# Score tiles in an attention kernel: three in every step, one of them from two half-wide matmuls in one bank, ordered through GpSimd

## The chip, the core and the metric

The kernel runs on one core of a Trainium2 chip. The core has five engines with their own instruction queues: TensorE (PE; its weight loads are listed apart as PEld), VectorE (DVE), ScalarE (ACT), GpSimd (POOL) and SyncE (SP), which here only issues DMAs. PE writes into PSUM, eight banks of 128 partitions by 512 float32; DVE and ACT read it. The metric is device time in microseconds (us), the median of several runs.

## The reference

One input x (2048 tokens by 512 features) is normalised and goes through two branches, which are multiplied and added to x:

```python
xn = _layernorm(x)
qkv = (xn @ wqkv).reshape(B, S, 3, H, Dh).transpose(2, 0, 3, 1, 4)   # H = 32 heads of Dh = 16
scores = einsum("bhqd,bhkd->bhqk", q, k) * Dh ** -0.5
o = einsum("bhqk,bhkd->bhqd", softmax(scores), v)
s = o.transpose(0, 2, 1, 3).reshape(B, S, D) @ wo
g = silu(einsum("bsf,fd->bsd", gelu(xn @ w1 + b1), w2) + b2)          # F = 1376
return x + s * g
```

## The kernel before, in words

All is float32; products with weights are made from a high and a low part, three matmuls in place of one. Attention works on 32 **units** u: eight groups of four heads times four chunks of 512 queries.

The softmax needs each query's largest score first, so each unit's scores are made twice.

- **S tiles** (line 174): 128 queries by 512 keys of one head, one matmul of 48 contraction rows into one bank; DVE takes the row maximum (line 176). 64 S tiles make a unit, 2048 in all. The maxima of a unit are reduced (line 188, `nmh` and `nm`), a low part is subtracted on POOL (line 189), transposed on PE (line 200), copied (line 208) and sent through DRAM into two extra rows of the queries (`load_mh`).
- **T tiles** (line 654): 128 keys by 512 queries with 50 rows, the two extra ones subtracting the maximum; ACT takes the exponential (line 656) out of PSUM.
- **V matmuls** (line 723): the four heads' exponentials times their values, eight instructions that use all four column groups of PE and accumulate over 16 key blocks in one bank. ACT copies that bank to `os` (line 730) at a unit's end; later DMAs, a reciprocal on DVE and a multiply on POOL (`o_div`, line 760) divide by the sum.

Heads come in two kinds, a = 0 and a = 1: their rows lie at partitions 0 and 64. An S or T matmul uses only one half of PE's rows, so two of them, one on each half, run side by side. The V matmuls use all rows.

In the first stage (LayerNorm, projections, the gated MLP) S tiles of the first units are put between other matmuls by `fill`, 4 x LEAD = 560 of them. Then comes a loop of 513 **steps** n, which holds the attention. Step n makes the four T tiles of key block n mod 16 of unit n // 16, the V matmuls of step n - 1, and some S tiles of later units. `due(n)` says how many S tiles are to be made by then; the difference to those made (three, in some steps four, none from about step 492 on) picks a string from ORDER:

```python
ORDER = {0: "TTTTV", 1: "TTTTSV", 2: "TTTSTSV", 3: "STTTSTSV", 4: "STTSTSVTS"}
```

T tiles alternate a = 0, 1, 0, 1; the S tiles take the other half than the tile ahead of them, as long as neither kind is four ahead. The order of work on each engine is the order in which the program writes it; waits between engines follow from the tiles. `todo` (filled by `at`) hangs other work on a step: loads of queries and of the next group's keys (`load_k`, on POOL's queue, `pos=0` being behind the first T of a step, `pos=3` behind the last), `o_move`, `o_den`, `o_div`, the output weights (`load_wo`, `split_wo`), and near the end the output matmuls (`w_mul`, line 77).

PSUM: S tiles use three banks in turn (two of `ps_s`, and whichever of `ps_x` and `ps_v` does not hold the V sum of this unit); T tiles use four (three of `ps_t`, one of `ps_m`). In the first stage S tiles have the two banks of `ps_s`.

`mark` in the first stage shows how two row halves that add into one bank are ordered: an ACT instruction waits for the matmul of the one half, and the matmul of the other half waits for it (`add_manual_dep`).

Of the kernel before, what the change touches and what calls it, by code (L numbers as in the profile page):

```python
# [27 lines left out]
GH = 4  # L28
# [3 lines left out]
VW = DH + 1  # L32
LEAD = 140
NW = 10
# [4 lines left out]
W2B = 2  # L39
ORDER = {0: "TTTTV", 1: "TTTTSV", 2: "TTTSTSV", 3: "STTTSTSV", 4: "STTSTSVTS"}  # L40
KB = 3
# [5 lines left out]
def fused(ctx: ExitStack, tc: tile.TileContext, x, wqk, wv, wo, w1, b1, w2, b2, out):  # L47
# [3 lines left out]
    keep = ctx.enter_context(tc.tile_pool(name="keep", bufs=1))  # L51
    ps_s = ctx.enter_context(tc.tile_pool(name="ps_s", bufs=2, space=PSUM))
    ps_x = ctx.enter_context(tc.tile_pool(name="ps_x", bufs=1, space=PSUM))
# [27 lines left out]

    QS, QT, MX, NM, MH = {}, {}, {}, {}, {}
    qss = []
    NU = NG * NCH

    s_ring = [ps_s, ps_s]
    s_turn = [0]
    end_tile = lambda: s_tile()

    def s_tile(shape=(P, CH)):  # L90
        pool = s_ring[s_turn[0] % len(s_ring)]
        s_turn[0] += 1
        return pool.tile(list(shape), F32, name="pv" if pool is ps_v else "ps")

# [50 lines left out]

    def load_mh(u):
        for a in range(2):
            nc.sync.dma_start(QT[u][64 * a + 48:64 * a + 50].bitcast(F32), mh_d[u, :, a::2, :])

    halves = [[(u, st, p) for u in range(NU) for st in range(NCH * NCH) for p in range(2)] for _ in range(2)]  # L150
    made = [0, 0]
    ended = [0]
    later, errands = [], []

# [4 lines left out]
    def flush():  # L159
        while later and later[0][0] <= 0:  # L160
            u = later.pop(0)[1]
            s_end1(u)
            s_end2(u)

    def s_one(a):
        u, st, p = halves[a][made[a]]
        made[a] += 1
        g = u // NCH
        qi, ki = divmod(st, NCH)
        if u not in MX:  # L170
            MX[u] = qring.tile([P, GH, NCH, NCH], F32, name="mx")
        ps = s_tile()
        r, q = slice(64 * a, 64 * a + 3 * DH), QS[u]
        nc.tensor.matmul(ps, q[r, p, qi * P:(qi + 1) * P],  # L174
                         kts[g % KB][p][r, ki * CH:(ki + 1) * CH], start=True, stop=True)
        nc.vector.tensor_reduce(MX[u][:, 2 * p + a, qi, ki:ki + 1], ps, axis=AX.X, op=OP.max)  # L176
        if min(made) == 32 * (ended[0] + 1):
            v = ended[0]
            ended[0] += 1
            s_end0(v)  # L180
            later.append([12 if "seen" in prog else 8, v])

    def s_end0(u):
        nm = qring.tile([P, GH * NCH], F32, name="nm")
        NM[u] = qring.tile([P, 2, GH * NCH], F32R, name="nmh")
        mx = MX.pop(u).rearrange("p a b c -> p (a b) c")
        for dst in (NM[u][:, 0], nm):
            nc.vector.tensor_reduce(dst, mx, axis=AX.X, op=OP.max, negate=True)  # L188
        nc.gpsimd.tensor_sub(NM[u][:, 1], nm, NM[u][:, 0].bitcast(F32))  # L189
# [8 lines left out]
    def s_end1(u):  # L198
        pm = end_tile()
        nc.tensor.matmul(pm[:2 * GH * NCH, :P], NM.pop(u).rearrange("p i a -> p (i a)"), ident_r, start=True, stop=True)  # L200
        MH[u] = pm

    def s_end2(u):
        mh = qring.tile([2 * GH * NCH, P], F32, name="mh")
# [4 lines left out]
        nc.sync.dma_start(mh_d[u].rearrange("i j (q s) -> (i j q) s", s=P), mh)  # L209

    sa = ExitStack()
# [109 lines left out]
    with ExitStack() as s1:  # L321
# [4 lines left out]
        def a_tile(shape):  # L326
            banks[0] += 1
            i = banks[0] % 6
            if i < 2:
                return ps_s.tile(list(shape), F32, name="ps")  # L330
            if i == 2:
                return ps_x.tile(list(shape), F32, name="ps")
            return ps_t.tile(list(shape), F32, name="pst")
# [139 lines left out]

    SYNC = mybir.DependencyInfo(mybir.DependencyClass.Sync, mybir.DependencyReason.DATA)
    prog.update(n=0, pe=0, seen=0)
# [163 lines left out]
    def t_tile():  # L639
        turns[0] += 1  # L640
        if turns[0] < 5:
            pool = (ps_m, ps_x, ps_s, ps_s)[turns[0] - 1]
# [46 lines left out]
    s_ring.append(ps_x)  # L689
    s_turn[0] = 2  # L690
    qz.close()
# [15 lines left out]

    def split_wo(k):
        nc.gpsimd.tensor_copy(wo_h[:, k], WR[k])
        nc.gpsimd.tensor_sub(wo_l[:, k], WR.pop(k), wo_h[:, k].bitcast(F32))  # L710

    PV, OS, DN, DR = {}, {}, {}, {}
    def pv_pool(u):
        return (ps_v, ps_x)[u % 2]

    def pv_step(u, k):
        g = u // NCH
        if k == 0:
            pool = pv_pool(u)
            PV[u] = pool.tile([P, CH], F32, name="pv" if pool is ps_v else "ps")  # L720
        for j in range(GH):
            h = (g * GH + j) * VW
            nc.tensor.matmul(PV[u][32 * j:32 * j + 32, :], vsb[:, k, h:h + 32], PT[u, k][:, j, :],  # L723
                             start=(k == 0), stop=(k == NT - 1))
        del PT[u, k]
        if k == NT - 1:
            OS[u] = wb.tile([P, CH], F32, name="os", bufs=1)
            pv = PV.pop(u)
            if u < NU - 1:
                nc.scalar.activation(OS[u], pv, AF.Copy)  # L730
# [75 lines left out]
    def w_mul(t, ks, parts=(0, 1)):  # L806
        if t not in PW:
            PW[t] = [ps_t.tile([P, CH], F32, name="pst") if NW <= t < NT - NCH or i else
                     ps_m.tile([P, CH], F32, name="ps") if t == NT - 1 else s_tile()
                     for i, cs in enumerate(cols(t))]  # L810
# [28 lines left out]
    def due(n):  # L839
        return min(4 * L, 4 * LEAD + max(0, (4 * (L - LEAD) * n - 300) // (DONE - 1)))  # L840

    for u in range(NU):
        g, c = divmod(u, NCH)
        if c == 0 and g == KB:
            at(57, load_k, g, range(6), nc.gpsimd, 0, S // 2, pos=0)
            at(64, load_k, g, range(6), nc.gpsimd, S // 2, S // 2, pos=0)
        elif c == 0 and g > KB:
            for i in range(6):
                at(64 * (g - KB + 1) + 6 + i, load_k, g, (i,), nc.gpsimd, pos=0)
        if u >= 2:  # L850
            at(16 * u - 14, load_qt, u)
            need = min(n for n in range(L) if due(n) >= 64 * (u + 1)) + (4 if u < NU - 1 else 2)
            at(max(16 * u - 14, need), load_mh, u)
        if u < NU - 1:
            at(16 * u + 17, o_move, u, pos=0)
            at(16 * u + (25 if g < NG - 1 else 19), o_den, u, pos=0)
            at(16 * u + (31 if g < NG - 1 else 22), o_div, u, nc.gpsimd)
    T3 = range(NT - NCH, NT)
    last, late = 1, range(NW, NT)
    for t in range(NW):  # L860
# [13 lines left out]
    for k in range(KT):  # L874
        at(104 + 16 * k, load_wo, k)
        at(112 + 16 * k, split_wo, k)
    for n in range(L + 1):
        ua, ka = divmod(n, 16)
        want = due(n) - sum(made)
        i = 0  # L880
        if n > 1 and (n - 1) % 16 == 0:
            s_ring[:] = [ps_s, ps_s, pv_pool((n - 1) // 16 + 1)]
            s_turn[0] = 0
        for op in ORDER[want] if n > 1 else ("TTTTV", "TTTVTSS")[n]:
            if op == "S":
                h = 1 - last if made[1 - last] - made[last] < 4 and made[1 - last] < 2 * L else last
                s_one(h)
                last = h
            elif op == "V":
# [68 lines left out]
```

## Time and profile before

| | |
|---|---|
| median of 3 runs | 1640.5 us (1640.18 to 1640.83) |
| the profiled execution | 1640.26 us, of it the profile's span 1638.5 us |
| granted clock of TensorE | 0.999 |
| PE busy | 1627.3 us (99%) |
| DVE busy | 1389.8 us (85%) |
| ACT busy | 1271.9 us (78%) |
| POOL busy | 373.5 us (23%) |
| first V load, last V load | 483.4 us, 1614.0 us |

Rows of a timeline give the start, the length, the engine, the line, the operation, the tile written and the tiles read, and the count of instructions merged into the row; in brackets stands how long the engine was idle before and what ended that. Matmuls are pipelined: a row's length is more than the time until the next can follow, and the ends are modelled. The first stage ends near 483 us; the loop of steps fills most of what follows, and 20 steps without S tiles and the last output tiles make the end.

### The profile page before, as it was taken

The numbers are of one execution on the slowest core, as the hardware profiler recorded it, in microseconds if no ns is written. First come the engines' busy times: TensorE is split into PE (matmuls) and PEld (weight loads), VectorE is DVE, ScalarE is ACT, GpSimd is POOL, SyncE is SP. The second block draws the span as 40 slices with busy tenths as digits, with TensorE's granted clock in tenths as the row PEclk, the third lists the DMA queues.
The fourth block names the chain that finished last, engine by engine and source line by source line (L and its number), as shares of the span: only waits on it lengthen the run. The fifth ranks groups of instructions, "written<-read, shape, count | busy, mean of one in ns | idle before, by whom it ended". The sixth has DMA issues, their size and how long they took to land.

```text
span 1638.5 us, 31026 instructions
## 1 busy us (share of the span) xinstructions
PE 1627.3 (99%) x11656; PEld 898.3 (55%) x11656; DVE 1389.8 (85%) x2299; ACT 1271.9 (78%) x2523; POOL 373.5 (23%) x366
## 2 busy tenths in 40 slices
PE   9999999999999999999999999999999999999998
PEld 7898999988974434333334443433334443434445
DVE  7299999999988888888888888888888888888733
ACT  4333433434349999999999999999999999999984
POOL 4235565756630011001000100100100000000144
PEclk9999999999999999999999999999999999999999
DMA  6625334453330122112301411411141111110152
GB/s 200 147 72 150 113 118 130 138 135 121 111 117 26 29 50 47 31 45 49 61 26 28 79 29 28 66 31 31 36 59 32 28 28 37 32 28 22 56 191 94
DMA packets 76214, 116.83 MB, mean 71 GB/s; under 512 B 24964, under 2 KB 26244, under 8 KB 74696
## 3 DMA queue, kind: packets, MB, share of 16 engines
q1 hardware_dynamic: 72604, 102.42, 22.3%
q0 software_dynamic: 3264, 12.35, 4.5%
q8 instruction: 92, 1.51, 0.4%
q14 instruction: 58, 0.48, 0.1%
q10 hardware_dynamic: 196, 0.07, 0.0%
HBM read 84.35 MB, written 25.97 MB: 67 GB/s over the span
## 4 chain that ended last, share of the span: by engine, by line
PE 94%; DVE 2%; issue 2%; ACT 1%; POOL 1%; DMA 0%; SPq 0%; ACTq 0%; DVEq 0%; POOLq 0%
PE ps L174 23%; PE pv L723 15%; PE ps L723 15%; PE ps L506 12%; PE pst L654 12%; PE pst L506 7%; PE pv L174 3%; PE ps L77 2%; PE pv L506 2%; ACT slot L656 1%; PE pst L77 1%; POOL ol L791 1%; DVE mx L176 0%; PE ps L654 0%; POOL gx L824 0%
## 5 line engine op out<-in xcount | busy, mean ns | idle before, releaser
L176 DVE TENSOR_REDUCE mx<-ps 128x1 f32<-128x512 f32 x1808 | 1168.6, 685 | 160.3 <-PE ps L654 76.6
L656 ACT ACTIVATE slot<-pst 128x512 f32<-128x512 f32 x1533 | 806.9, 608 | 5.0 <-PE ps L174 4.5
L656 ACT ACTIVATE slot<-ps 128x512 f32<-128x512 f32 x515 | 308.7, 600 | 44.4 <-PE ps L654 9.8
L174 PE MATMUL ps<-kt,slot 48*128 48x512 f32 x864 | 327.9, 443 | 0.0
L174 PEld LDWEIGHTS ps<-kt,slot 48*128 48x128 f32 x864 | 158.2, 184 | 256.8 <-DVE mx L176 235.6
L654 PE MATMUL pst<-qt,kt 50*128 50x512 f32 x1149 | 294.1, 409 | 0.4 <-DVE gt L587 0.3
L723 PE MATMUL pv<-slot,vsb 128*32 128x512 f32 x2048 | 272.7, 605 | 0.0
L723 PE MATMUL ps<-slot,vsb 128*32 128x512 f32 x2048 | 272.5, 604 | 0.0
L506 PE MATMUL ps<-slot,w1h 64*128 64x512 f32 x1088 | 225.2, 394 | 0.4 <-ACT junk L519 0.4
L174 PE MATMUL ps<-kt,qz 48*128 48x512 f32 x512 | 211.1, 416 | 0.2
L654 PE MATMUL ps<-qt,kt 50*128 50x512 f32 x387 | 189.8, 492 | 0.0
L176 DVE TENSOR_REDUCE mx<-pv 128x1 f32<-128x512 f32 x240 | 163.8, 683 | 11.6 <-PE ps L654 7.8
L174 PE MATMUL ps<-slot,slot 48*128 48x512 f32 x432 | 166.2, 441 | 0.2
L506 PEld LDWEIGHTS ps<-slot,w1h 64*128 64x128 f32 x1088 | 153.8, 185 | 9.5 <-ACT junk L519 2.3
L654 PEld LDWEIGHTS pst<-qt,kt 50*128 50x128 f32 x1149 | 144.5, 186 | 21.5 <-issue 8.4
L506 PE MATMUL ps<-slot,w1l 64*128 64x512 f32 x544 | 154.0, 393 | 0.0
L174 PEld LDWEIGHTS ps<-slot,slot 48*128 48x128 f32 x432 | 78.6, 184 | 115.0 <-DVE mx L176 104.8
L307 POOL TENSOR_TENSOR hl<-hg,hh 128x512 fp32r<-128x512 f32 x76 | 96.9, 1297 | 129.2 <-ACT hh L306 80.8
L189 POOL TENSOR_TENSOR nmh<-nm,nmh 128x16 fp32r<-128x16 f32 x32 | 7.1, 221 | 497.9 <-DVE nm L188 266.5
L519 ACT ACTIVATE junk<-ident_r 1x1 f32<-1x1 f32 x91 | 17.8, 196 | 120.4 <-PE pst L506 104.0
L174 PEld LDWEIGHTS ps<-kt,qz 48*128 48x128 f32 x512 | 93.7, 183 | 11.8 <-DVE mx L176 2.7
L654 PE MATMUL pst<-qt,slot 50*128 50x512 f32 x384 | 97.7, 406 | 0.0
(161 smaller groups left out, 1980.7 us busy)
## 6 DMA issues: line engine op xcount, KB each, us to landing
raw<-in_w SPq DMA_DIRECT2D x88, 256.0 KB
qk_h<-hh SPq DMA_DIRECT2D x32, 256.0 KB
qk_l<-hl SPq DMA_DIRECT2D x32, 256.0 KB
qt<-qk_h SPq DMA_DIRECT2D x128, 64.0 KB
slot<-qk_h SPq DMA_DIRECT2D x96, 64.0 KB
xt<-in_x SPq DMA_DIRECT2D x16, 256.0 KB
g_d<-gt POOLq DMA_DIRECT2D x16, 256.0 KB, 3.7
qt<-qk_l SPq DMA_DIRECT2D x64, 64.0 KB
```

The lines of the kernel that those rows point to most:

```text
L77: nc.tensor.matmul(ps, lhs[a], rhs[b], start=first and n == 0, stop=last and n == 2)
L174: nc.tensor.matmul(ps, q[r, p, qi * P:(qi + 1) * P], kts[g % KB][p][r, ki * CH:(ki + 1) * CH], start=True, stop=True)
L176: nc.vector.tensor_reduce(MX[u][:, 2 * p + a, qi, ki:ki + 1], ps, axis=AX.X, op=OP.max)
L189: nc.gpsimd.tensor_sub(NM[u][:, 1], nm, NM[u][:, 0].bitcast(F32))
L307: nc.gpsimd.tensor_sub(hl, raw, hh.bitcast(F32))
L506: i = nc.tensor.matmul(ps, lhs[r], rhs[r], start=first, stop=last).ins
L519: i = nc.scalar.activation(junk[:, :1], ident_r[:1, :1].bitcast(F32), AF.Copy).ins
L654: nc.tensor.matmul(ps, kts[g % KB][p][r, k * P:(k + 1) * P], QT[u][r, p, :], start=True, stop=True)
L656: nc.scalar.activation(PT[u, k][:, 2 * p + a, :], ps, AF.Exp, scale=SCALE)
L723: nc.tensor.matmul(PV[u][32 * j:32 * j + 32, :], vsb[:, k, h:h + 32], PT[u, k][:, j, :], start=(k == 0), stop=(k == NT - 1))
L791: lo.tensor_sub(ol[:, :n], src, oh[:, :n].bitcast(F32))
```

## The change

Every step from the second to number 491 now makes exactly three S tiles, in one fixed order:

- **Two whole S tiles** (`S`), a = 0 and then a = 1 of the same pair of heads.
- **X and Y**: a third pair of heads is spread over two steps, half of the keys in each. X is a 256-wide matmul of a = 0 into the left half of a bank, Y a 256-wide one of a = 1 into its right half. One bank then holds both, and one DVE reduction takes the maximum of each half. Because two row halves write one bank, a `nop` on GpSimd waits for X, and Y waits for that `nop`. The bank is taken out of the ring of three at X and put back at Y.
- All S reductions now give two maxima (one for each 256 keys), and the unit's reduction (`nm`, `nmh`) takes 128 columns in place of 64.
- T tiles come as a = 1, 1, 0, 0, in all steps, those without S tiles too.
- The first stage makes 4 x 144 = 576 S tiles, nine whole units; `due` then adds three a step.
- The V sum's bank trades places with the third of the ring every 16 steps; its copy `os` is split for all units, left half on ACT, right half on DVE.
- The transposed maxima of a unit in the loop (`s_end1`) take a bank of the T tiles' ring.
- On POOL's queue: the subtraction of line 189 is written behind the next `nop` (`put_off`), the key loads are issued one piece a step, behind the fourth T, and the two halves of `split_wo` stand four steps apart.

```diff
-LEAD = 140
+LEAD = 144
...
-ORDER = {0: "TTTTV", 1: "TTTTSV", 2: "TTTSTSV", 3: "STTTSTSV", 4: "STTSTSVTS"}
+ORDER = {0: "TTTTV", 3: "TXSTTSTYV"}
+HC = CH // 2
...
+    def s_mm(ps, job, a, c0, k0, w):
+        u, st, p = job
+        qi, ki = at_of(job)
...
+        r = slice(64 * a, 64 * a + 3 * DH)
+        k0 += ki * CH
+        return nc.tensor.matmul(ps[:, c0:c0 + w], QS[u][r, p, qi * P:(qi + 1) * P],
+                                kts[u // NCH % KB][p][r, k0:k0 + w], start=True, stop=True).ins
+
+    def s_max(ps, job, heads, parts):
...
+        nc.vector.tensor_reduce(MX[u][:, 2 * p:2 * p + 2, qi, ki][:, heads, parts], ps.rearrange("p (n c) -> p n c", c=HC), axis=AX.X, op=OP.max)
+        done[u] += 1
+        if done[u] == 64:
+            s_end0(u)
+            later.append([12 if "seen" in prog else 8, u])
+
+    def s_whole(job, a):
+        ps = s_tile()[0]
+        s_mm(ps, job, a, 0, 0, CH)
+        s_max(ps, job, a, slice(0, 2))
...
+    def s_op(op):
+        if op == "S":
+            if whole:
+                s_whole(whole.pop(), 1)
+            else:
+                whole.append(jobs.pop(0))
+                s_whole(whole[0], 0)
+        elif op == "X":
+            if not cut:
+                cut[:] = [jobs.pop(0), 0]
+            ps, pool = s_tile(True)
+            x = s_mm(ps, cut[0], 0, 0, cut[1] * HC, HC)
+            token = nc.gpsimd.nop().ins
+            tc.add_manual_dep(token, x.name, SYNC, reason="row tile done")
+            cut[2:] = [ps, pool, token]
+            run_off()
+        else:
+            job, n, ps, pool, token = cut
+            y = s_mm(ps, job, 1, HC, n * HC, HC)
+            tc.add_manual_dep(y, token.name, SYNC, reason="other row tile")
+            s_max(ps, job, slice(0, 2), n)
+            s_ring.append(pool)
+            cut[1] += 1
+            if n:
+                cut.clear()
...
-        nc.gpsimd.tensor_sub(NM[u][:, 1], nm, NM[u][:, 0].bitcast(F32))
+        put_off.append(lambda: nc.gpsimd.tensor_sub(NM[u][:, 1], nm, NM[u][:, 0].bitcast(F32)))
...
-        pm = end_tile()
+        pm = s_tile()[0] if "seen" in prog else t_tile()
...
-            if u < NU - 1:
-                nc.scalar.activation(OS[u], pv, AF.Copy)
-            else:
-                nc.scalar.activation(OS[u][:, :CH // 2], pv[:, :CH // 2], AF.Copy)
-                nc.vector.tensor_copy(OS[u][:, CH // 2:], pv[:, CH // 2:])
+            nc.scalar.activation(OS[u][:, :HC], pv[:, :HC], AF.Copy)
+            nc.vector.tensor_copy(OS[u][:, HC:], pv[:, HC:])
...
-        return min(4 * L, 4 * LEAD + max(0, (4 * (L - LEAD) * n - 300) // (DONE - 1)))
+        return min(4 * L, 4 * LEAD + max(0, 3 * n - 1))
...
-            s_ring[:] = [ps_s, ps_s, pv_pool((n - 1) // 16 + 1)]
-            s_turn[0] = 0
+            v_pool[0], s_ring[2] = s_ring[2], v_pool[0]
...
-                    t_one(ua, ka, i // 2, i % 2)
-                    last = i % 2
+                    t_one(ua, ka, i % 2, 1 - i // 2)
```

More of the change, by code (lines that the diff above doesn't have):

```diff
@@ L146, in load_mh @@
     def load_mh(u):
+        assert u in sent
         for a in range(2):
             nc.sync.dma_start(QT[u][64 * a + 48:64 * a + 50].bitcast(F32), mh_d[u, :, a::2, :])
-    halves = [[(u, st, p) for u in range(NU) for st in range(NCH * NCH) for p in range(2)] for _ in range(2)]
+    heads = [(u, st, p) for u in range(NU) for st in range(NCH * NCH) for p in range(2)]
     made = [0, 0]
-    ended = [0]
-    later, errands = [], []
+    done = {u: 0 for u in range(NU)}
+    later, errands, sent = [], [], set()
     def tick():
@@ L165, in s_one @@
     def s_one(a):
-        u, st, p = halves[a][made[a]]
         made[a] += 1
[L168 to L181, printed above, removed]
+        s_whole(heads[made[a] - 1], a)
+    jobs, whole, cut, put_off = [], [], [], []
+    def s_op(op):
[13 more added lines that the diff above has]
+            cut[2:] = [ps, pool, token]
+            run_off()
+        else:
[3 more added lines that the diff above has]
+            s_max(ps, job, slice(0, 2), n)
+            s_ring.append(pool)
+            cut[1] += 1
+            if n:
+                cut.clear()
@@ L855, in fused @@
             at(16 * u + 17, o_move, u, pos=0)
-            at(16 * u + (25 if g < NG - 1 else 19), o_den, u, pos=0)
-            at(16 * u + (31 if g < NG - 1 else 22), o_div, u, nc.gpsimd)
+            at(16 * u + (25 if u < NU - 2 else 19), o_den, u, pos=0)
+            at(16 * u + (31 if u < NU - 2 else 22), o_div, u, nc.gpsimd)
     T3 = range(NT - NCH, NT)
-    last, late = 1, range(NW, NT)
+    late = range(NW, NT)
     for t in range(NW):
```

72 lines of the change are left out of this document (41 added, 31 removed).

## The prediction

> **What bounds the kernel now.** I read the page's busy times first, then the table by windows, then the timeline of single steps.
>
> ```profile
> span 1638.5 us, 31026 instructions
> PE 1627.3 (99%) x11656; PEld 898.3 (55%) x11656; DVE 1389.8 (85%) x2299; ACT 1271.9 (78%) x2523; POOL 373.5 (23%) x366
> PE 94%; DVE 2%; issue 2%; ACT 1%; POOL 1%; DMA 0%; SPq 0%; ACTq 0%; DVEq 0%; POOLq 0%
> 200.00:400.00 200.00, 199.83 (x1653) 180.50 (x1652) 184.48 (x288) 79.04 (x178) 125.23 (x109) 1.00 0.44 130
> 1000.00:1200.00 200.00, 199.90 (x1395) 80.16 (x1396) 178.54 (x302) 192.91 (x376) 13.55 (x22) 1.00 0.26 46
> ```
>
> The last two rows are windows of the first and of the attention stage (PE, PEld, DVE, ACT, POOL busy, granted clock 1.00). PE carries 94% of the chain. A busy PE row hides gaps, and DVE and ACT are nearly full beside it, so the steps themselves must be read. Here is one step, and the load that opens the next.
>
> ```profile
> 1074.12 0.16 PEld L723 LDWEIGHTS ps<-slot,vsb 128*32 128x32 f32 x8 [0.24 <-issue]
> 1075.11 0.50 PE L174 MATMUL ps<-slot,slot 48*128 48x512 f32 x1
> 1075.12 0.49 PE L654 MATMUL ps<-qt,kt 50*128 50x512 f32 x1
> 1075.45 0.39 PE L654 MATMUL pst<-qt,kt 50*128 50x512 f32 x2
> 1075.65 1.29 DVE L176 TENSOR_REDUCE mx<-ps 128x1 f32<-128x512 f32 x2 [0.59 <-PE ps L654]
> 1075.68 0.60 ACT L656 ACTIVATE slot<-ps 128x512 f32<-128x512 f32 x1
> 1075.68 0.39 PE L174 MATMUL ps<-slot,slot 48*128 48x512 f32 x1
> 1075.69 0.47 PE L174 MATMUL pv<-slot,slot 48*128 48x512 f32 x1
> 1075.91 0.40 PE L654 MATMUL pst<-qt,kt 50*128 50x512 f32 x1
> 1076.17 1.57 ACT L656 ACTIVATE slot<-pst 128x512 f32<-128x512 f32 x3
> 1076.24 0.16 PEld L723 LDWEIGHTS ps<-slot,vsb 128*32 128x32 f32 x8 [0.37 <-issue]
> 1076.85 0.68 DVE L176 TENSOR_REDUCE mx<-pv 128x1 f32<-128x512 f32 x1
> 1077.23 0.18 PEld L174 LDWEIGHTS ps<-slot,slot 48*128 48x128 f32 x1 [0.84 <-DVE mx L176]
> ```
>
> Seven tiles (three S of line 174, four T of line 654) run in pairs on the two row halves and begin at 0, 0.34, 0.57 and 0.80 us: four slots of 0.23, the first with 0.11 of weight load ahead. The V matmuls load 0.33 after the last slot began (its 0.23 and 0.10 of drain), and the next step opens 0.99 after that. That makes 2.12 us. Seven tiles fill three and a half slots, but one half gets four tiles and the other three, so half a slot of one row half is empty. The 0.84 that PEld "waits for DVE" is the V phase: that reduce had ended long before. What a slot is worth shows where the V comes early, at a step with four S:
>
> ```profile
> 486.74 0.16 PEld L723 LDWEIGHTS pv<-slot,vsb 128*32 128x32 f32 x8 [0.24 <-issue]
> ...
> 1021.86 0.16 PEld L723 LDWEIGHTS ps<-slot,vsb 128*32 128x32 f32 x8 [0.36 <-issue]
> 1023.76 0.16 PEld L723 LDWEIGHTS ps<-slot,vsb 128*32 128x32 f32 x8 [0.27 <-issue]
> 1026.50 0.16 PEld L723 LDWEIGHTS ps<-slot,vsb 128*32 128x32 f32 x8 [0.25 <-issue]
> ...
> 1546.85 0.16 PEld L723 LDWEIGHTS pv<-slot,vsb 128*32 128x32 f32 x8 [0.37 <-issue]
> ```
>
> From V to V: 1.90 with six tiles (three slots), then 2.74 with nine, against 2.12 with seven. So a slot less is worth 0.22 and PE does set the step. The first and last row bound the 489 steps that the change rewrites: 1060.1 us, 2.168 each.
>
> **The change part by part.**
>
> *The step.* It gets T X S T T S T Y V: on one half T, T, S and a 256-wide Y, on the other X, S, T, T. Both have three and a half slots. By the slot pitch alone V is due at 0.11 + 3.5 x 0.23 + 0.10 = 1.015 and the step lasts 1.015 + 0.99 = 2.005. That is PE's floor; two loops lie above it.
>
> *DVE's loop.* Three banks serve three score tiles, and X holds one from the step's start until Y is reduced. The second S takes the bank that the previous step's Y left. S0 streams from 0.225 (behind X's half slot) and lands 0.39 later at 0.615. DVE begins 0.04 after a landing (1075.61 to 1075.65), its pitch is 1.29 - 0.68 = 0.605, so S0, S1 and Y are reduced from 0.655, 1.26 and 1.865, and the last ends at 2.545. A load follows its releaser by 0.05 (next fence: os ends 1073.64, load 1073.69). So S1's load comes at 2.595 - T in its own step of length T, where PE would have it by 0.46. Behind it come 0.11 of load, its slot, Y's half slot and the drain: V is due 0.11 + 0.23 + 0.115 + 0.10 = 0.555 after the load, and T = 0.99 + 0.555 + 2.595 - T, hence T = 2.07. Two neighbouring steps share 4.14.
>
> *ACT's loop.* The first T lands at 0.50, ACT begins at 0.57, pitch (1.57 - 0.60)/2 = 0.485, so the fourth exp ends at 0.57 + 1.455 + 0.60 = 2.625. The next step's last T needs that bank: load at 2.675 - T, V 0.11 + 0.23 + 0.10 after it, and T = (0.99 + 0.44 + 2.675)/2 = 2.05. DVE's loop decides; ACT is 0.02 behind it.
>
> So 489 x 2.07 = 1012.2. The 14 or so early-V pairs (1.90 + 2.74 against 2 x 2.12, 0.4 each) are gone with the even three tiles, which the difference to 1060.1 contains.
>
> *Change of the V bank every 16 steps* (30 times).
>
> ```profile
> 1071.65 1.06 PE L723 MATMUL pv<-slot,vsb 128*32 128x512 f32 x8
> ...
> 1073.01 0.63 ACT L730 ACTIVATE os<-pv 128x512 f32<-128x512 f32 x1
> ...
> 1073.69 0.18 PEld L174 LDWEIGHTS pv<-slot,slot 48*128 48x128 f32 x1 [0.31 <-ACT os L730]
> ```
>
> The third S waits for the whole copy os; that step, V at 1071.65 to V at 1074.12, lasts 2.47. Halves on ACT and DVE free the bank sooner, but now the second S needs it: ACT is free for its half at 2.025 + 0.485 - 2.07 = 0.44, the half takes 0.32 to 0.63, say 0.40, and S1 loads at 0.89 in place of 0.525. That is 0.37 against 0.35: 30 x 0.37 = 11.1.
>
> *End of a unit* (23 in these steps).
>
> ```profile
> 1092.62 0.22 DVE L188 TENSOR_REDUCE nmh<-mx 128x16 fp32r<-128x64 f32 x1
> 1092.76 0.21 DVE L188 TENSOR_REDUCE nm<-mx 128x16 f32<-128x64 f32 x1
> ...
> 1093.11 0.22 POOL L189 TENSOR_TENSOR nmh<-nm,nmh 128x16 fp32r<-128x16 f32 x1 [22.44 <-DVE nm L188]
> ...
> 1094.02 0.25 PE L200 MATMUL ps<-ident_r,nmh 128*32 128x128 f32 x1
> ...
> 1094.19 0.18 PEld L654 LDWEIGHTS pst<-qt,kt 50*128 50x128 f32 x1
> ```
>
> The small transpose puts the step's first load off by 0.17 and keeps doing so, 23 x 0.17 = 3.9; its bank comes from T's ring, and the copy out of it is done before the fourth T needs the bank. The two nm reduces, hidden in DVE's idle time today, come into its loop with twice the columns. By their lengths they take at most 0.43 and the added columns some 0.14 more (0.68 - 0.22 for 448 columns is 0.001 for each); they start 0.14 apart, so 0.28 + 0.14 = 0.42 is likelier. DVE would idle 2.07 + 0.655 - 2.47 = 0.255 in a step; the rest, 0.16, is late: 23 x 0.16 = 3.7.
>
> *The token through POOL.*
>
> ```profile
> L189 POOLq EVENT_SEMAPHORE  x23: 17/17/43, 116.1 to 1553.0; - x23
> 1096.51 1.28 POOL L760 TENSOR_TENSOR slot<-slot,dn 64x512 f32<-64x512 f32 x1 [3.18 <-DMA dn<-den_d]
> ```
>
> X lands at 0.11 + 0.115 + 0.16 = 0.385. POOL follows a DVE result by 0.14 (1092.97 to 1093.11). The nop itself has no row: below it lies the 17 ns (median) that an event wait takes in POOL's queue, above it POOL's smallest instruction, 0.22 (line 189, above). Back to PE I take 0.05. So the token is there at 0.59 to 0.80. Y's load is late only after 0.755 (S1's stream ends at 0.865, the load takes 0.11). I take the 17 ns row, which like a nop moves no data, so no cost, with 0.16 to spare. The Trainium skill, PSUM — Partial Sum Buffer, section "Engine vs sequencer instructions", says that a nop is run by the sequencer and not by the engine behind it. By that the token is early and the sum stands; by POOL's smallest instruction it would be 1638 (worked out under the rivals); nothing in the trace of before shows a nop.
>
> *POOL's other work.* The 1.28 us multiplies, the wo pieces (now two, four steps apart) and the k loads (one piece a step) come after their step's nop: 0.6 + 1.28 is 1.9, and the next X lands at 2.45. In before a multiply began at 1096.51, in step 283 counted along the V loads, four steps ahead of its place in the program (step 287), so its DMA is there. The moved nmh subtraction is needed two steps later. Cover gone, each would cost up to 1.3; I count 0. S0 needs the bank of S1's reduce, done at 1.945 of the step before: free.
>
> *The tail.* In the last 20 steps there are no S, and T's order is now half, half, other, other.
>
> ```profile
> 1581.61 0.18 PEld L654 LDWEIGHTS ps<-qt,kt 50*128 50x128 f32 x1 [0.84 <-ACT slot L783]
> 1581.61 0.29 PEld L654 LDWEIGHTS pst<-qt,kt 50*128 50x128 f32 x3
> 1582.27 0.19 PEld L77 LDWEIGHTS pv<-wo_h,oh 128*128 128x128 f32 x1 [0.36 <-PE ps L654]
> ```
>
> Two pairs take 0.66. Issued in the new order only the middle two tiles overlap: three slots, 0.23 more, 20 x 0.23 = 4.6. Nothing covers it, since the output matmuls follow on PE.
>
> *LEAD 140 to 144.* 16 more S in the first stage. There PE is full and DVE at 92%: half a slot for each of 16 is 1.8; all exposed on DVE 16 x 0.605 = 9.7; nothing at the least. I take 2, as PEld waits for DVE hardly at all there:
>
> ```profile
> PEld ps L174 <- DVE mx L176: 3.5, 11, 0.5
> ```
>
> *The sum.* 1012.2 + 11.1 + 3.9 + 3.7 = 1030.9 against 1060.1: -29.2. With +4.6 and +2 it is -22.6. The profiled execution took 1640.3 us around its span of 1638.5, 0.2 under the median of 1640.5; so 1617.
>
> **The rivals.**
>
> *PE's floor.* The loops close a little earlier than reckoned (a 0.07 shorter sum of landing, reduce and release on both) and T is 2.005 to 2.03. For it: six-tile steps do reach 1.90. Against: DVE's third reduce then ends 0.54 into the next step. 489 x 2.005 = 980.4, which gives 1617 - 32 = 1585.
>
> *The token comes late: slower.* Y then waits at the head of PE's queue with all of V behind it. With 0.22 for the nop the token comes at 0.795, V at 0.795 + 0.11 + 0.115 + 0.10 = 1.12, T = 2.11: 20 us more, 1638. If besides X's landing is told only with that of the first T issued before it (0.50 in place of 0.385), T is 2.225: 1617 + 76 = 1693. The decisive point is a token at 0.80, where the whole gain is lost. For it: the rows of a pair end together in issue order. Against: with 17 ns for the nop even that token comes at 0.71. The Trainium skill, TensorE: Matmul & The Clock Gate, section "The mechanism", has matmuls start and end strictly in program order, which is the case of 0.50; all tiles of before are equally wide, so no run here shows it yet.
>
> *No gain.* DVE's reduce into two columns costs 0.04 more, or ACT and DVE disturb each other's loops, and T is 2.09 to 2.13: 1627 to 1647.
>
> **How the numbers follow.** Forecast (T 2.04 to 2.09, 1602 to 1627): 0.45. PE's floor: 0.18. No gain: 0.17, most of it still under 1637. Late token: 0.20, most of it above 1640. A difference of 0.2% (3.3 us) is about what can be told from none. Faster: 0.63, with 0.10 of "no gain" and 0.02 of the token 0.75. Same: 0.04 and 0.01 of these two, 0.05. Slower: 0.03 and 0.17, 0.20. The range runs from the floor at 1585 to 1660, between the two prices of the late token; beyond it I leave about 0.15.
>
> **What would show it.** V to V near 2.07 on average, alternating or with PEld waiting about 0.1 for DVE before the second S. Y's load not waiting for POOL. V to V 2.005 flat: the floor. A PEld wait on POOL each step: the late token. T phase 0.89 in the tail. Wrong altogether, if POOL's queue stalls on a DMA and Y with it, or if a 256-wide matmul costs more than half a slot.

## The result, and the profile after

The changed kernel takes 1635.5 us (median of 7 runs, 1634.48 to 1635.88), the kernel before 1640.4 beside it. The ratio is 0.9969 (0.9957 to 0.9980): 0.3% faster, 4.9 us where 22.6 were forecast. The profiled execution took 1635.6 us.

The page of the changed kernel: span, busy times of the engines, shares of the chain that ended last.

```profile
span 1633.7 us, 32521 instructions
PE 1605.2 (98%) x12146; PEld 928.8 (57%) x12146; DVE 1406.8 (86%) x2330; ACT 1255.7 (77%) x2522; POOL 371.8 (23%) x366
PE 92%; ACT 4%; DVE 2%; issue 1%; DMA 0%; ACTq 0%; POOL 0%; SPq 0%; DVEq 0%; POOLq 0%
```

Shares hardly move (PE 94% to 92% of the chain), so the page alone doesn't tell where the gain went. The V loads do. They cut the span into three parts:

| part | before | after | difference | forecast |
|---|---|---|---|---|
| start to the second step's V load | 486.74 | 497.15 | +10.4 | +2 |
| 489 steps | 1060.11 | 1041.98 | -18.1 | -29.2 |
| after step 491's V load | 91.65 | 94.57 | +2.9 | +4.6 |
| span | 1638.5 | 1633.7 | -4.8 | -22.6 |

Sorting the 489 distances from V load to V load by length splits the middle part:

| steps | mean | forecast mean | sum | forecast |
|---|---|---|---|---|
| 436 plain | 2.063 | 2.07 | 899.7 | 902.5 |
| 23 at a unit's end | 2.41 | 2.40 | 55.3 | 55.2 |
| 30 with a change of the V bank | 2.90 | 2.44 | 87.0 | 73.2 |

Now the rows. This is a timeline of the changed kernel: a plain step, the step with the change of the V bank two steps on, and the two steps behind the last S tile.

```profile
999.53 0.16 PEld L773 LDWEIGHTS ps<-slot,vsb 128*32 128x32 f32 x8 [0.20 <-issue]
1000.52 0.18 PEld L704 LDWEIGHTS ps<-qt,kt 50*128 50x128 f32 x1 [0.84 <-ACT slot L706]
1001.11 0.18 PEld L180 LDWEIGHTS pv<-slot,slot 48*128 48x128 f32 x1 [0.17 <-DVE mx L186]
1001.22 0.19 PEld L180 LDWEIGHTS ps<-slot,slot 48*128 48x128 f32 x1
1001.66 0.16 PEld L773 LDWEIGHTS ps<-slot,vsb 128*32 128x32 f32 x8 [0.25 <-issue]
1003.67 0.16 PEld L773 LDWEIGHTS ps<-slot,vsb 128*32 128x32 f32 x8 [0.20 <-issue]
...
1004.67 0.18 PEld L704 LDWEIGHTS ps<-qt,kt 50*128 50x128 f32 x1 [0.84 <-ACT slot L706]
1005.12 0.41 ACT L779 ACTIVATE os<-ps 128x256 f32<-128x256 f32 x1
1005.56 0.42 DVE L780 COPY os<-ps 128x256 f32<-128x256 f32 x1 [0.37 <-ACT os L779]
1006.04 0.18 PEld L180 LDWEIGHTS ps<-slot,slot 48*128 48x128 f32 x1 [0.96 <-DVE os L780]
1006.58 0.16 PEld L773 LDWEIGHTS ps<-slot,vsb 128*32 128x32 f32 x8 [0.25 <-issue]
...
1539.13 0.16 PEld L773 LDWEIGHTS ps<-slot,vsb 128*32 128x32 f32 x8
1542.74 0.16 PEld L773 LDWEIGHTS ps<-slot,vsb 128*32 128x32 f32 x8 [0.36 <-issue]
1543.84 1.26 POOL L838 TENSOR_TENSOR ol<-slot,oh 128x512 fp32r<-128x512 f32 x1 [3.76 <-ACT oh L837]
1545.06 0.22 POOL L239 TENSOR_TENSOR nmh<-nm,nmh 128x16 fp32r<-128x16 f32 x1
1545.33 0.11 PEld L252 LDWEIGHTS pst<-ident_r,nmh 128*32 128x32 f32 x1 [2.44 <-POOL nmh L239]
1549.50 0.16 PEld L773 LDWEIGHTS ps<-slot,vsb 128*32 128x32 f32 x8 [0.65 <-issue]
```

*Plain steps.* V to V is 2.13, then 2.01. In the long one the second S's load (1001.11) waits 0.17 for DVE; Y's load (1001.22) follows it and waits for nothing. That alternation and that wait are DVE's loop as forecast.

*The change of the V bank.* The step opens at 1004.67. ACT's half of the copy ends at 1005.53, DVE's half starts only then, held for 0.37, and ends at 1005.98; the second S loads at 1006.04, 1.37 after the opening where 0.89 was forecast. V to V is 2.91.

*Behind the last S.* The step from 1542.74 lasts 6.76. Its head is the small transpose of the last unit (line 252), whose load comes after 2.44, released by the subtraction on POOL (line 239); 0.84 of the 2.44 is the V phase, as in every step, and the other 1.6 is the wait. The subtraction stands behind an output subtraction of 1.26 (line 838) in POOL's queue. Behind this wait comes a second loss: the clock granted to TensorE falls to 0.50.

```profile
1546.40:1548.00 1.60, 1.60 (x4) 1.16 (x4) 0.00 (x0) 1.60 (x4) 0.00 (x0) 0.50 0.05 10
```

This row has the columns of the windows below. The output matmuls follow each other by 0.43 there instead of 0.23. Nine kernels of this document have that wait in their profiles. Only this one and that of the run with shorter reductions in the first stage show such a stretch behind it, of 3.4 us by the trace's clock records; in the other seven the step lasts 5.2 to 5.6. So about 1.5 of the 6.76 comes with the clock and belongs to this execution.

*The first stage.* The windows of 300 us in it, of the kernel before and of the changed one (PE, PEld, DVE, ACT, POOL busy with counts, granted clock, DMA share and GB/s):

```profile
100.00:400.00 300.00, 299.83 (x2481) 270.93 (x2479) 277.41 (x431) 117.03 (x265) 181.28 (x156) 1.00 0.45 130
```

```profile
100.00:400.00 300.00, 299.73 (x2427) 272.58 (x2428) 276.52 (x431) 112.70 (x256) 174.66 (x149) 1.00 0.43 126
```

PE counts as full in both, yet it makes 54 matmuls fewer in the same time. DVE makes exactly as many reductions, 431, at 276.5/431 = 0.64 us of its busy time each. So it is DVE's count that time goes by there.

### The profile page after: what moved, and what is told of

The parts are those of the page before. It is cut to its first block, busy times and chain, and to the rows that moved or that the text cites. A ratio compares the mean times of both kernels' runs of the same rounds, so it can differ in the third digit from the quotient of the medians.

```text
span 1633.7 us, 32521 instructions
## 1 busy us (share of the span) xinstructions
PE 1605.2 (98%) x12146; PEld 928.8 (57%) x12146; DVE 1406.8 (86%) x2330; ACT 1255.7 (77%) x2522; POOL 371.8 (23%) x366
## 4 chain that ended last, share of the span: by engine, by line
PE 92%; ACT 4%; DVE 2%; issue 1%; DMA 0%; ACTq 0%; POOL 0%; SPq 0%; DVEq 0%; POOLq 0%
PE ps L773 21%; PE ps L180 14%; PE pst L704 14%; PE ps L556 12%; PE pv L773 8%; PE pst L556 7%; PE ps L704 5%; PE ps L79 3%; PE pv L180 3%; ACT slot L706 3%; PE pv L556 2%; PE pst L79 1%; DVE os L780 1%; ACT os L779 1%; DVE slot L74 0%
## 5 line engine op out<-in xcount | busy, mean ns | idle before, releaser
L186 DVE TENSOR_REDUCE mx<-ps 128x2 f32<-128x512 f32 x1685 | 1096.9, 685 | 121.7 <-PE ps L180 80.3
L773 PE MATMUL ps<-slot,vsb 128*32 128x512 f32 x2944 | 392.1, 605 | 0.0
L704 PE MATMUL pst<-qt,kt 50*128 50x512 f32 x1149 | 378.2, 429 | 0.4 <-DVE gt L637 0.3
L180 PE MATMUL ps<-kt,slot 48*128 48x256 f32 (+1 forms) x1036 | 325.2, 374 | 8.2 <-DVE os L780 8.2
L186 DVE TENSOR_REDUCE mx<-pv 128x2 f32<-128x512 f32 x363 | 248.1, 684 | 18.5 <-PE pv L180 14.0
L773 PE MATMUL pv<-slot,vsb 128*32 128x512 f32 x1152 | 153.2, 604 | 0.8 <-DVE gx L866 0.8
L180 PE MATMUL ps<-slot,slot 48*128 48x256 f32 (+1 forms) x442 | 140.4, 375 | 3.7 <-DVE os L780 3.1
L180 PE MATMUL pv<-kt,slot 48*128 48x512 f32 (+1 forms) x328 | 123.1, 375 | 3.1 <-DVE os L780 3.0
L569 ACT ACTIVATE junk<-ident_r 1x1 f32<-1x1 f32 x90 | 17.7, 196 | 134.1 <-PE pst L556 128.4
L704 PEld LDWEIGHTS ps<-qt,kt 50*128 50x128 f32 x387 | 71.2, 184 | 67.5 <-ACT slot L706 52.8
L773 PEld LDWEIGHTS ps<-slot,vsb 128*32 128x32 f32 x2944 | 57.9, 108 | 84.0 <-issue 83.7
```

Of the source, the lines that this page charges most:

```text
L180: return nc.tensor.matmul(ps[:, c0:c0 + w], QS[u][r, p, qi * P:(qi + 1) * P], kts[u // NCH % KB][p][r, k0:k0 + w], start=True, stop=True).ins
L186: nc.vector.tensor_reduce(MX[u][:, 2 * p:2 * p + 2, qi, ki][:, heads, parts], ps.rearrange("p (n c) -> p n c", c=HC), axis=AX.X, op=OP.max)
L569: i = nc.scalar.activation(junk[:, :1], ident_r[:1, :1].bitcast(F32), AF.Copy).ins
L704: nc.tensor.matmul(ps, kts[g % KB][p][r, k * P:(k + 1) * P], QT[u][r, p, :], start=True, stop=True)
```

## The experiments

**The copy of the V bank, whole on DVE.** My theory was that the 2.90 comes from the two halves running one after the other. The rival was that the second S is held by DVE's reductions, and a longer copy on DVE makes it worse. The edit, all units but the last:

```diff
-            nc.scalar.activation(OS[u][:, :HC], pv[:, :HC], AF.Copy)
-            nc.vector.tensor_copy(OS[u][:, HC:], pv[:, HC:])
+            if u < NU - 1:
+                nc.vector.tensor_copy(OS[u], pv)
+            else:
...
```

> The changed kernel, but the V sum's copy os is one instruction on DVE (512 wide) in every unit but the last. Theory (the two half copies read one bank and run one after the other, ACT's first): the copy starts on DVE about 0.40 us after the step opens and takes 0.68, so the second S loads at about 1.13 in place of 1.36, and the step at a change of the V bank takes about 2.68 from V to V in place of 2.90: 30 x 0.22 = 6.6 us less, about 1629 us. Rival (the step is long because the V sum changes its bank, or because ACT is behind): 2.90 stays, 1634 to 1637 us.

Measured: 1629.0 us, ratio 0.9934 (0.9920 to 0.9949). The timeline of a step with a change, which opens at 1002.50:

```profile
1002.93 0.68 DVE L780 COPY os<-ps 128x512 f32<-128x512 f32 x1
1003.67 0.18 PEld L180 LDWEIGHTS ps<-slot,slot 48*128 48x128 f32 x1 [0.76 <-DVE os L780]
```

The second S loads at 1.17 in place of 1.37, although DVE now copies twice as much. The step with a change is 2.71. One copy of 0.68 beats two of 0.41 and 0.42, the second of which waits for the first.

**The same, whole on ACT.**

```diff
...
+            if u < NU - 1:
+                nc.scalar.activation(OS[u], pv, AF.Copy)
+            else:
...
```

> The changed kernel, but os is one instruction on ACT (512 wide) in every unit but the last, as it was before. Theory (serial halves): the copy runs on ACT from about 0.45 to 1.08 after the step opens, the second S loads at about 1.13, V to V about 2.68, and DVE is spared 0.42: about 1629 us; ACT's four exponentials are put off by 0.63, which may cost the next step up to 0.2, so up to 1635. Rival (ACT is the bound there and the half on DVE relieves it): longer than 2.90, above 1637 us.

Measured: 1627.7 us, ratio 0.9923 (0.9907 to 0.9940). The step with a change is 2.66.

```profile
1003.71 0.63 ACT L780 ACTIVATE os<-ps 128x512 f32<-128x512 f32 x1
1004.39 0.18 PEld L180 LDWEIGHTS ps<-slot,slot 48*128 48x128 f32 x1 [0.71 <-ACT os L780]
```

30 x (2.90 - 2.66) = 7.2 of the 7.8 us won. Halving the copy was the fault, whichever engine takes the whole. A whole copy still leaves the step 0.60 (ACT) or 0.65 (DVE) above a plain one.

**The kernel before with LEAD = 144.** This does one part of the change alone, in the old kernel.

```diff
-LEAD = 140
+LEAD = 144
```

> The kernel before, with LEAD 144 in place of 140 and nothing else: 16 more S tiles in the first stage. Theory (in the first stage each S tile costs a whole turn of DVE's reduce with two banks, 0.65 us): the first V load moves from 483.4 to about 494 us; in the loop the steps with four S are gone (15 x 0.4 = 6 us less), so about 1644 us. Rival (the 10 us of the first stage come from the two-column reductions or the longer unit reductions): first V load at 484 to 486 us and 1635 to 1638 us in all.

Measured: 1644.1 us, ratio to the kernel before 1.0024 (1.0014 to 1.0033). The V loads of this run, first and last start:

```profile
L723 PEld LDWEIGHTS pv<-slot,vsb x2048: 105/108/111, 493.8 to 1569.3; 128*32 128x32 f32 x187
```

The first V load comes at 493.8 instead of 483.4: 10.4 us for 16 tiles, 0.65 each, which is the price of a DVE reduction there (0.64). The old loop, which has fewer S left to make, gives some 6.5 of it back (1644.1 against 1640.2). In the changed kernel they stand whole in the first part of the table above.

**The first stage with shorter reductions.** Is it DVE's pace alone that holds the first stage? In it, 192 of each 256 scores are reduced and the rest is left out (the exponent's scale is divided by 64 so that nothing overflows).

```diff
-        ... ps.rearrange("p (n c) -> p n c", c=HC), ...
+        ... ps.rearrange("p (n c) -> p n c", c=HC)[:, :, :192 if "seen" in prog else HC], ...
```

> The changed kernel, but in the first stage each DVE reduction reads only the first 192 of each 256 scores, so the first nine units' maxima leave a quarter of the keys out (and the exponential's scale is divided by 64 to keep it finite). Theory (in the first stage an S tile's turn through two banks, of which the reduction is the longest part, sets the pace): 576 turns shorter by up to 0.13, the first V load moves from 493.5 to 425 to 470 us. Rival (PE's own matmuls set the pace of the first stage, and 16 more S tiles cost PE 10 us): first V load within 5 us of 493.5.

Measured: 1620.6 us. Its V loads and a window of the first stage:

```profile
L773 PEld LDWEIGHTS pv<-slot,vsb x1152: 105/108/111, 478.5 to 1594.7; 128*32 128x32 f32 x192
```

```profile
200.00:400.00 200.00, 199.75 (x1675) 174.26 (x1673) 154.29 (x297) 78.51 (x180) 126.91 (x111) 1.00 0.44 131
```

The first V load comes 15.0 us sooner, not as early as expected (425 to 470): with DVE relieved (154 of 200 us busy) another limit takes over, only 15 us below. DVE's waits between 150 and 450 us point to PE. This is the largest of them; in the changed kernel it is 5.7 us, 22 times.

```profile
DVE mx L186 <- PE ps L556: 25.0, 90, 0.5
```

So both are near their limit there: a tile more costs what DVE takes, a tile's reduction less soon runs into PE. No run relieved PE.

**The loop with shorter reductions.** The counterpart: 192 of each 256 scores reduced in the loop of steps, the rest left out, with the same smaller scale.

```diff
-        ... ps.rearrange("p (n c) -> p n c", c=HC), ...
+        ... ps.rearrange("p (n c) -> p n c", c=HC)[:, :, :HC if "seen" in prog else 192], ...
```

> The changed kernel, but in the loop each DVE reduction reads only the first 192 of each 256 scores, so the maxima leave a quarter of the keys out (and the exponential's scale is divided by 64 to keep it finite). Theory (DVE's loop through the bank of Y makes every second step 2.12): the reduction takes about 0.55 in place of 0.68, the pitch 0.47, the second S waits no more, and V to V is flat between PE's floor of 2.00 and ACT's loop of 2.05: 1605 to 1625 us. Rival (the alternation comes from ACT's banks or from the token): 2.01 and 2.12 stay and the time is 1633 to 1636 us.

Measured: 1620.2 us. The timeline, two steps and a reduction:

```profile
1000.26 0.16 PEld L773 LDWEIGHTS ps<-slot,vsb 128*32 128x32 f32 x8 [0.25 <-issue]
1002.27 0.16 PEld L773 LDWEIGHTS ps<-slot,vsb 128*32 128x32 f32 x8 [0.20 <-issue]
1002.39 0.55 DVE L186 TENSOR_REDUCE mx<-pv 128x2 f32<-128x384 f32 x1
```

Neighbouring steps take 2.01 and 2.06, a mean of 2.035 against 2.063. With 0.13 off each reduction DVE's loop is out of the way, and the step falls by about 0.03 only: the next limit lies just below, between PE's floor (2.005) and the 2.05 reckoned for ACT's loop. Which of the two it is was not told apart.

**The token made by an instruction of POOL's engine.** In place of the `nop`, a memset of one element that nobody reads.

```diff
...
-            token = nc.gpsimd.nop().ins
+            token = nc.gpsimd.memset(mhw2, 0.0).ins
```

> The changed kernel, but the token is POOL's smallest real instruction, a memset of one element, in place of the nop. Theory (the token is far from late: the nop's round trip leaves some 0.1 to 0.2 us): with 0.05 to 0.2 us more, Y's load waits 0 to 0.1 us, V to V rises by at most 0.05, so 1635 to 1655 us, and PEld shows waits on POOL before Y. Rival (the token is what makes 2.12): every step longer by the whole of the instruction, 1680 us and more.

Measured: 1650.0 us, V to V 2.10 flat. The timeline of a step that opens at 1001.48:

```profile
1001.48 0.18 PEld L705 LDWEIGHTS pst<-qt,kt 50*128 50x128 f32 x1 [0.84 <-ACT slot L707]
1002.13 0.09 POOL L216 MEMSET mhw<- 1x1 f32 x1 [2.01 <-PE ps L181]
1002.27 0.18 PEld L181 LDWEIGHTS ps<-slot,slot 48*128 48x128 f32 x1
```

Y's load comes at 0.79 instead of 0.70. The memset, 0.09 long, starts 0.65 after the opening, and 0.05 after its end Y loads. At 0.79 the token decides the step, which the prediction had put at 0.755. So the `nop` of the changed kernel is just early enough, and "late token" is a real danger: this kind of late costs 14.5 us (a single run).

**Y asked for early.** When does the `nop`'s token arrive? In the changed kernel nothing waits for it. Put Y ahead of the second S, and PE does.

```diff
-ORDER = {0: "TTTTV", 3: "TXSTTSTYV"}
+ORDER = {0: "TTTTV", 3: "TXSTTYSTV"}
```

> The changed kernel with Y ahead of the second S (T X S T T Y S T V), so that S, not Y, is the last on its row half, and the token is needed at 0.46 us after the step opens in place of 0.75. Theory (DVE's loop sets 2.07, and the token arrives near 0.59): the load of Y then shows the token's arrival; DVE's loop falls to about 2.03, but Y waits 0.13 and with it V: V to V 2.08 to 2.14, 1640 to 1670 us. If the token comes by 0.46: 2.02 to 2.05, 1612 to 1625 us.

Measured: 1680.3 us, V to V 2.18 flat, more than expected. The timeline of a step, from its first load to V, and the row of the waits between 800 and 1400 us:

```profile
1001.32 0.18 PEld L704 LDWEIGHTS pst<-qt,kt 50*128 50x128 f32 x1 [0.84 <-ACT slot L706]
1001.96 0.18 PEld L180 LDWEIGHTS ps<-kt,slot 48*128 48x128 f32 x1 [0.23 <-POOLq L215]
1002.51 0.16 PEld L773 LDWEIGHTS pv<-slot,vsb 128*32 128x32 f32 x8 [0.25 <-issue]
```

```profile
PEld ps L180 <- POOLq L215: 59.8, 269, 0.2
```

Y loads 0.64 after the opening, having waited 0.23 for POOL: this is the token's arrival. From there the rest follows in a row: 0.11 of load, half a slot of 0.115, S's slot of 0.23 and 0.10 of drain put V at 1.195, and with 0.99 the step is 2.185.

**X ahead of the T.** If X landed at 0.385 as forecast, a token at 0.64 means 0.255 for the way over POOL. If X is told done only with the T that was issued ahead of it (0.50), the way takes 0.14. Issue X first and the two part. Y stays early, as in the run before.

```diff
-ORDER = {0: "TTTTV", 3: "TXSTTSTYV"}
+ORDER = {0: "TTTTV", 3: "XTSTTYSTV"}
```

> Y ahead of the second S as in y_early, and X ahead of the first T (X T S T T Y S T V). In y_early Y's load, freed by the token, came 0.64 us after the step opened. Theory (X's end is told only with that of the T issued ahead of it, 0.50 in place of 0.385): with X first the load of Y comes about 0.11 earlier, at 0.53, and V to V falls from 2.18 to about 2.07. Rival (X's end is told when it lands, and the round trip through POOL takes 0.25): Y's load stays at 0.62 to 0.65 and V to V at 2.16 to 2.18.

Measured: 1625.7 us, V to V 2.04 flat.

```profile
1003.54 0.18 PEld L180 LDWEIGHTS ps<-slot,slot 48*128 48x128 f32 x1 [0.84 <-DVE mx L186]
1004.03 0.18 PEld L180 LDWEIGHTS ps<-slot,slot 48*128 48x128 f32 x1
1004.57 0.16 PEld L773 LDWEIGHTS ps<-slot,vsb 128*32 128x32 f32 x8 [0.25 <-issue]
```

Y loads at 0.49, so it was the T. Could it be the count alone? POOL waits for a number of ended matmuls, which needs T's end too when T is ahead. The trace records when that semaphore goes up, and excludes it: with T first the first two increments come at 0.51 and 0.55 after the opening, with X first at 0.40 and 0.51 (medians of 360 steps). If X told its end on landing and only the count held POOL back, there would be an increment near 0.40 in both. From X's increment to Y's load the way over POOL takes 0.09 in both runs (0.55 to 0.64, 0.40 to 0.49); from the reckoned landings it would be 0.14 and 0.105. That order also ends the alternation, and the step comes within 0.035 of PE's floor. By the order, DVE reduces Y ahead of the second S, so that Y's bank is free earlier for the next step's second S; this is inferred, the rows show only the flat 2.04.

**The old T order in the steps without S.**

```diff
-                    t_one(ua, ka, i % 2, 1 - i // 2)
+                    t_one(ua, ka, *((i % 2, 1 - i // 2) if want else (i // 2, i % 2)))
```

> The changed kernel, but in the 20 steps without S tiles the four T alternate between the row halves again (1, 0 in place of the pairs). Theory (PE lets the second half's T run beside the first ones, whatever the order in the program): V to V stays 3.25 and the time within 1 us of 1635.5. Rival (the prediction's term, three slots in place of two, hidden in the last steps by something else): 3 to 5 us less.

Measured: 1635.6 us, ratio to the kernel before 0.9975 (0.9965 to 0.9985), against 0.9969 for the changed kernel: no difference. The order costs nothing. In the changed kernel's timeline the four loads look like those of before:

```profile
1557.02 0.18 PEld L704 LDWEIGHTS ps<-qt,kt 50*128 50x128 f32 x1 [0.84 <-ACT slot L706]
1557.02 0.29 PEld L704 LDWEIGHTS pst<-qt,kt 50*128 50x128 f32 x3
1557.68 0.19 PEld L79 LDWEIGHTS pv<-wo_h,oh 128*128 128x128 f32 x1 [0.36 <-PE pst L704]
```

The T phase takes 0.66, as before, not 0.89; the steps take 3.25 in both.

**The end mended, with the copy on ACT.** Two edits beside that of the copy: the last unit's subtraction is written to POOL at once, and in steps without S the V bank trades places with the ring's first bank.

```diff
-        if "seen" in prog:
+        if "seen" in prog or u == NU - 1:
             run_off()
...
-            v_pool[0], s_ring[2] = s_ring[2], v_pool[0]
+            z = 2 if want else 0
+            v_pool[0], s_ring[z] = s_ring[z], v_pool[0]
```

> The changed kernel with the whole os on ACT, with the last unit's subtraction on POOL written at once and not put off, and with the V sum in the steps without S tiles moved to the bank of the ring that was used longest ago. Theory (the 6.76 step behind the last S tile is PE waiting for that subtraction, which stands behind the output's subtraction in POOL's queue; the 4.12 step is V waiting for DVE's read of the bank just used): both steps near 3.25 to 4.3, 2 to 4 us under the 1627.7 of the kernel with os on ACT alone: about 1624.5. Rival (the maxima's way through DRAM sets these steps): 1627 to 1628 us.

Measured: 1625.5 us, ratio 0.9911 (0.9896 to 0.9927), 2.2 below the copy alone; the two edits were not run apart. The timeline behind the last S:

```profile
1534.56 0.22 POOL L239 TENSOR_TENSOR nmh<-nm,nmh 128x16 fp32r<-128x16 f32 x1 [0.84 <-PE ps L704]
1536.39 0.16 PEld L773 LDWEIGHTS ps<-slot,vsb 128*32 128x32 f32 x8 [0.36 <-issue]
1537.39 0.11 PEld L252 LDWEIGHTS pst<-ident_r,nmh 128*32 128x32 f32 x1 [0.84 <-issue]
```

The subtraction is done 2.6 us before the transpose, which no longer waits for it. The two steps behind the last S take 3.6 and 3.63, and the later step with a change of the V bank takes 3.26, where the kernel with the copy alone has 4.11.

**All of it together.** The copy whole, the end mended, and X first with Y early; once with the copy on ACT, once on DVE.

```diff
-ORDER = {0: "TTTTV", 3: "TXSTTSTYV"}
+ORDER = {0: "TTTTV", 3: "XTSTTYSTV"}
```

> The kernel with os on ACT and the two repairs behind the last S tile (1625.5 us), with the order X T S T T Y S T V in addition. Theory (the order moves DVE's last reduction ahead of its deadline, as in x_first: 2.04 flat in place of 2.07 on average): some 440 plain steps x 0.03 = 13 us less, the steps at a unit's end up to 0.1 longer, so 1612 to 1617 us. Rival (os on ACT and the order get in each other's way through ACT's loop): 1618 to 1626 us.

> The same with os on DVE. Theory: DVE has more idle time in a step now that its last reduction is not late, so os costs as little there as on ACT: within 2 us of the kernel with os on ACT. Rival (DVE's loop is still the tighter one): 3 to 6 us slower than that.

Measured: 1613.4 us with ACT, ratio 0.9834 (0.9820 to 0.9847), and 1616.9 with DVE, ratio 0.9856 (0.9843 to 0.9870). The page and timeline of the one with ACT:

```profile
span 1611.5 us, 32452 instructions
...
1000.25 0.16 PEld L773 LDWEIGHTS ps<-slot,vsb 128*32 128x32 f32 x8 [0.25 <-issue]
1002.28 0.16 PEld L773 LDWEIGHTS ps<-slot,vsb 128*32 128x32 f32 x8 [0.24 <-issue]
1004.32 0.16 PEld L773 LDWEIGHTS ps<-slot,vsb 128*32 128x32 f32 x8 [0.24 <-issue]
```

Steps are 2.04 flat, those with a change of the V bank 2.54. The mended kernel wins 27.3 us, and with the copy on ACT it is 3.5 faster than on DVE.

## Why the prediction was right and wrong

The sign was right, the size was not: 1635.5 lies inside the range, 18.5 above the forecast. The differences by term: +8.4 from LEAD, +13.8 from the change of the V bank, -2.8 from plain steps, -1.7 at the end. These add to 17.7 of the 17.9 between the forecast for the profiled execution and its time. (By its own terms the sum is 1640.5 - 22.6 = 1617.9, put down as 1617; nothing hangs on it.)

**Right: DVE's loop, with the next limit close below.** Plain steps alternate and average 2.063 against 2.07, the second S waits 0.17 for DVE, and with DVE relieved the step stops at 2.035, near the 2.05 reckoned for ACT. The rival that DVE and ACT would disturb each other (2.09 to 2.13) fell, and so did PE's floor: DVE's loop does close where reckoned. That floor is nearly reached only with the other order (2.04).

**Right: the unit's end,** 2.41 for 2.40, where two estimates add up. Which of the two terms holds how much was not separated.

**Right in the outcome, wrong in a step: the token.** It costs nothing in the changed kernel. But "X lands at 0.385" is not what POOL hears. X's end is told behind that of the T issued ahead of it, at 0.55, and it was the quick `nop` that saved the sum: with Y early the token is there at 0.64 against 0.755, 0.11 to spare rather than 0.16. (POOL's own signal to PE comes at 0.60 after the opening, in that run and in the changed kernel alike.) The rival's two conditions were thus half met. The Trainium skill, TensorE: Matmul & The Clock Gate, section "The mechanism", has matmuls end strictly in program order; the 0.64 with T first and 0.49 with X first agree with that.

**Failed: "LEAD 140 to 144 ... I take 2".** It measured 10.4, beyond even the bound of 9.7. I priced a tile by PE's slot because PE's busy share was full and "PEld waits for DVE hardly at all". Both were misread. A busy PE row hides gaps, as the prediction itself says of the loop, and the waits on DVE that the view listed there, 3.5 us in all, were no measure of the pace that DVE set. The count of reductions in the two windows, the same before and after, shows that pace, but only once the second trace is there; the run with LEAD alone changed isolates the price.

**Failed: the change of the V bank, 0.37 over a plain step.** It measured 0.83. The halves were taken as running side by side on two engines. The row shows DVE's half held until ACT's has ended. The wait is on a semaphore, so the order is in the program. The Trainium skill, PSUM — Partial Sum Buffer, section "PSUM bank collisions raise a hardware error", has it that two engines must not access one bank in the same partition at once, and tells the author to guard by bank; the trace agrees in that the halves never overlap (1005.53, 1005.56), and no run here shows what an overlap would do. The profile of before had shown it once: there the copy was whole except for the last unit, and in that unit DVE's half waits for ACT's.

```profile
1615.21 0.39 ACT L732 ACTIVATE os<-ps 128x256 f32<-128x256 f32 x1 [1.23 <-PE ps L723]
1615.62 0.42 DVE L733 COPY os<-ps 128x256 f32<-128x256 f32 x1 [1.69 <-ACT os L732]
```

**Failed: the tail, +4.6.** It measured 0. "Only the middle two tiles overlap" assumed that the third T, on the free row half, can't start ahead of the second, which waits for its own half. The T phase is 0.66 with either order. TensorE's signals of the four ends come 0.52, 0.75, 0.78 and 0.81 after the opening at 1557.02, and 0.52, 0.55, 0.75 and 0.78 in the step of before at 1581.61: the third T starts early, and only its end is told behind the second's. The Trainium skill, TensorE: Matmul & The Clock Gate, section "The mechanism", also has matmuls start strictly in program order; by that the phase would be 0.89, so the trace does not bear that half of the rule out.

**Failed: POOL's other work at 0.** "The moved nmh subtraction is needed two steps later" held for every unit but the last, which has no later `nop` behind it in time. There the step of 6.76 costs 3.5 more than the 3.25 of before: some 2.0 by the late transpose, as the 5.2 of the other profiles shows, and 1.5 by the granted clock of 0.50. Another loss at the end was not foreseen either. Where the V bank changes in the tail, the next V waits for a DVE read of its new bank (4.12 in place of 3.25):

```profile
1563.37 0.16 PEld L773 LDWEIGHTS pv<-slot,vsb 128*32 128x32 f32 x8 [1.23 <-DVE gx L866]
```

Against these stand 0.74 and 0.15 won in two other steps behind the last S (4.35 to 3.61, 3.41 to 3.26); the remaining 0.6 us of that part were not traced. The part came out close to its forecast, +2.9 for +4.6, by luck: a cost that isn't there was forecast, and others that are there were not.

## What to carry to other kernels

When a trace with a few tiles more is at hand, price an added tile by the engine whose count of instructions per window stays the same in both, not by the one whose busy share is fullest: here 16 tiles cost DVE's 0.65 each on a PE that counted as 100% busy. Splitting one bank's copy between two engines shortens nothing if the second half waits for the first; look for that wait before halving a duration. When an operation is put off until "the next" of something, follow it to the last iteration, where there may be no next.

## What the runs showed of the hardware

- TensorE tells the end of a matmul only with those issued ahead of it, on the other row half too: the signal of the half-wide X came 0.15 us later with a T ahead of it (0.55 in place of 0.40; Y's load 0.64 in place of 0.49).
- The start is freer than the end: of four matmuls issued half, half, other, other, the third starts beside the first (both 1557.02), and the phase is as short as with alternate halves (0.66). The ends are told in the order of issue all the same.
- A `nop` that waits on GpSimd and releases TensorE takes 0.09 us from the signal of one matmul's end to the load of the next. With a memset of one element, 0.09 long, that load comes 0.15 later (0.79 in place of 0.64).
- Of nine profiles in which TensorE waits some 1.6 to 2.0 us behind the last S, two show the granted clock at 0.50 for 3.4 us soon after, with matmuls 0.43 apart in place of 0.23; in seven it stays at 1.00 there, and so it does in the three profiles without that wait. What decides between them isn't shown.
